# Last tokens of four batches multiplied as seven block products, and a new order of steps

## The chip, the core and the metric

The kernel runs on one core of a Trainium2 chip. The metric is device time of one execution in microseconds (us). A core has engines with queues of their own, each of which runs in the order written: TensorE (PE in the profile, with its weight loads as PEld), VectorE (DVE), ScalarE (ACT), GpSimd (POOL) and SyncE (SP), which only starts DMAs here. All arithmetic is in fp32.

## The reference

Eight batches of 576 tokens, 8 heads of 64 columns. Linear attention without a softmax, a normalisation of each head, then a gated unit with a causal convolution of 5 taps:

```
kv  = einsum('bhsd,bhse->bhde', k, v)
out = einsum('bhsd,bhde->bhse', q, kv)
x   = out / sqrt(mean(out*out, -1) + 1e-6) * g_norm      # heads joined: 576 x 512 per batch
gate = sigmoid(sum_k conv_w[k] * x[token - 4 + k])       # causal, per column
y   = (gate * (x @ w_val)) @ w_out                       # w_val, w_out: 512 x 512
```

## The kernel before

**Stages of one batch.** `kv_product` (PE) makes kv, `kv_copy` (ACT) takes it out of the PSUM bank. `load_q` and `turn_q` (SP, DVE) bring q turned over. `raw_pair` and `raw_tail` (PE, 64x64 tiles) multiply q by kv for chunks of 128 tokens, and for the last 64. `square` (ACT), `sums` (DVE) and `powers` (POOL) make the roots, `normalise` (ACT) scales the eight heads of a chunk. `turn_blocks` (DVE) turns the scaled chunk over in blocks and `move_blocks` carries four slices to x transposed (`xT`) by DMA, two from SP's queue and two from POOL's; the last 64 tokens go by `turn_x` (PE) and `keep_x` (ACT). `halo` (POOL) copies what the convolution needs from neighbours. `gate_start` (ACT), four `gate_tap` (DVE) and `gate_end` (ACT, sigmoid) make each of four column groups of the gate. `x_sums` (DVE), seven `val_fast` (PE) and `val_keep` (ACT and DVE) make x @ w_val from batch 2 on, as seven block products in place of eight. `gated` (DVE) multiplies by the gate; the product lies in `gv`.

**The output product.** Batches go in pairs i = 0 to 3. A batch's first 512 tokens are done in two groups of 256 tokens, so there are four groups p per pair. For each, a 2x2 block scheme takes seven products n = 0 to 6: `token_sums` (DVE) makes four sums of blocks of `gv` for both groups of a batch, `fast_product i p n` (PE) multiplies, `fast_keep` takes the results out of the banks: n = 0, 1, 2, 6 are ACT copies, n = 4 and 5 are DVE adds (n = 5 takes in product 3 as well). The last 64 tokens of both batches of a pair are multiplied plainly: `out_product i 8` (line 786) has 64 columns of weights on each half of the array, 512 columns wide, and `keep_out` copies the result. `store` sends each finished tile of 128 tokens with four DMAs. At the very end `store_part` and `store_last` split the last two tiles over SP's and ACT's queues.

**Order.** Nothing is scheduled automatically. `PLAN` is a list of some 1,250 steps, and each engine gets its instructions in the order of that list. `@ 1 4` behind a step names the buffers that it opens, out of rooms of fixed count (8 PSUM banks, 3 `w64` rooms for sums of tokens, 4 `ot` tiles for results, and so on). A wait arises where an engine reaches a step whose operands or buffer are not ready, and everything behind it on that engine waits too.

Of the kernel before, what the change touches and what calls it, by code (L numbers as in the profile page):

```python
# [43 lines left out]
narrow_weight wval 2 4; load_half k 2 1 @ 0; val_product 0 0 1 @ 2; keep_x 0 1; narrow_weight wout 1 5 @ 2;
keep_x 0 0; narrow_weight wval 2 7; narrow_weight wval 3 3; narrow_weight wout 1 0 @ 1;
narrow_weight wout 1 6 @ 0; gate_start 0 0 @ 0; kv_product 1 0; narrow_weight wval 3 4; gate_start 0 3 @ 1;
gate_tap 0 0 3; sort_q 1 2; turn_q_rows 1 4 @ 0; narrow_weight wval 3 7; val_product 0 0 0 @ 5; load_q 2 0;
gate_tap 0 0 2; keep_val 0 0 1; gate_tap 0 3 3; gate_start 0 1 @ 2; sort_q 1 4; val_sums 2;
val_product 0 3 0 @ 6; gate_tap 0 1 3; kv_copy 1 1; kv_copy 1 0; load_q 2 1; sort_q 1 0; gate_tap 0 0 1;
raw_tail 1 @ 0 2; gate_tap 0 3 2; raw_pair 1 3 @ 1 4; square 1 4 @ 2; narrow_weight wout 0 5 @ 3;  # L50
keep_val 0 0 0; gate_tap 0 0 0; val_product 0 2 1 @ 7; gate_start 0 2 @ 3; gate_tap 0 3 1; square 1 3 @ 0;
square 1 2 @ 1; sums 1 4 @ 1 1; gate_tap 0 2 3; narrow_weight wout 1 1; powers 1 4; load_half k 2 0 @ 0;
val_product 0 1 0 @ 5; sums 1 3; keep_val 0 1 1; stage_weight wout 3 @ 0; gate_end 0 0; gate_tap 0 1 2;
powers 1 3; narrow_weight wout 1 2; sums 1 2; narrow_weight wout 1 3; val_product 0 2 0 @ 3; gated 0 0;
keep_val 0 3 0; keep_val 0 2 1; gate_tap 0 2 2; normalise 1 4 @ 2; powers 1 2; narrow_weight wout 1 4;
normalise 1 3 @ 0; raw_pair 1 1 @ 7 6; turn_q 2 0 @ 0; stage_weight wout 2 @ 1; turn_q 2 2; turn_x 1 4 @ 0;
load_q 2 3; val_product 0 3 1 @ 2; gate_tap 0 3 0; keep_x 1 4; normalise 1 2 @ 1; gate_tap 0 2 1;
narrow_weight wout 0 6 @ 2; turn_x 1 3 @ 0; keep_val 0 3 1; gate_tap 0 1 1; load_q 3 1; turn_x 1 2 @ 1;
keep_val 0 1 0; square 1 1 @ 2; kv_product 2 0 @ 4 2; narrow_weight wout 0 0 @ 0; keep_x 1 3;
narrow_weight wout 1 7; keep_x 1 2; sums 1 1; kv_product 2 1; narrow_weight wout 0 1; gate_tap 0 1 0;  # L60
powers 1 1; square 1 0 @ 0; val_product 1 1 1 @ 5; narrow_weight wout 2 0 @ 1; load_half k 3 1 @ 0;
narrow_weight wout 0 2; narrow_weight wout 2 5 @ 1; load_half k 3 0 @ 0; narrow_weight wout 3 5 @ 3;
narrow_weight wout 0 3; sums 1 0; kv_copy 2 0; gate_tap 0 2 0; kv_copy 2 1; narrow_weight wout 2 1;
normalise 1 1 @ 2; powers 1 0; val_product 1 0 1 @ 0; narrow_weight wout 2 6 @ 0; narrow_weight wout 0 4;
turn_q 2 1; val_product 1 3 1 @ 1; halo 1; narrow_weight wout 2 2; narrow_weight wout 0 7; load_q 3 0;
keep_val 0 2 0; turn_q 2 3; keep_val 1 1 1; keep_val 1 0 1; weight_sums 0; normalise 1 0 @ 0; turn_x 1 1 @ 4;
load_q 3 2; narrow_weight wout 3 0 @ 0; raw_pair 2 3 @ 3 2; narrow_weight wout 3 6 @ 1; val_sums 0;
narrow_weight wout 2 3; raw_pair 2 1 @ 5 0; turn_q 3 1 @ 1; square 2 2 @ 1; turn_x 1 0 @ 6; square 2 3 @ 2;
narrow_weight wout 2 4; keep_x 1 1; val_product 1 2 1 @ 7; sums 2 2 @ 0 0; load_half v 3 0 @ 0; keep_x 1 0;
val_sums 1; gate_end 0 3; powers 2 2; load_half v 3 1 @ 0; sums 2 3; keep_val 1 3 1; gate_end 0 1; gated 0 3;  # L70
val_product 1 0 0 @ 4; gate_start 1 0 @ 0; narrow_weight wout 2 7; gate_end 0 2; powers 2 3; gated 0 1;
square 2 0 @ 0; gate_tap 1 0 3; val_product 1 1 0 @ 6; square 2 1 @ 1; turn_q 3 0; normalise 2 2 @ 1;
gated 0 2; load_q 3 3; val_product 1 2 0 @ 1; gate_tap 1 0 2; keep_val 1 2 1; keep_val 1 1 0; sums 2 1;
normalise 2 3 @ 2; load_q 4 0; turn_q 3 2; powers 2 1; val_product 1 3 0 @ 7; sums 2 0; narrow_weight wout 3 1;
token_sums 0 0 0 @ 2; keep_val 1 2 0; narrow_weight wout 3 2; turn_blocks 2 3; kv_product 3 0 @ 2 6;
powers 2 0; gate_tap 1 0 1; narrow_weight wout 3 3; token_sums 0 0 2 @ 1; keep_val 1 3 0;
fast_product 0 0 1 @ 3; normalise 2 1 @ 0; load_half k 4 0 @ 0; narrow_weight wout 3 4; token_sums 0 0 1;
fast_product 0 1 0 @ 1; turn_blocks 2 2; normalise 2 0 @ 2; fast_product 0 0 0 @ 7; turn_q 3 3; kv_product 3 1;
narrow_weight wout 3 7; load_q 4 2; fast_keep 0 0 1 @ 2; keep_val 1 0 0; token_sums 0 0 3; fast_keep 0 0 0 @ 3;
raw_tail 2 @ 0 5; gate_start 1 3 @ 1; turn_blocks 2 1; fast_product 0 0 3; square 2 4 @ 2; turn_blocks 2 0;  # L80
kv_copy 3 1; kv_copy 3 0; gate_start 1 1 @ 2; fast_product 0 1 1 @ 4; sums 2 4; move_blocks 2 0; weight_sums 1;
fast_keep 0 1 0 @ 0; raw_pair 3 1 @ 6 2; weight_sums 2; powers 2 4; gate_tap 1 1 3; move_blocks 2 2;
fast_product 0 0 2; gate_tap 1 0 0; move_blocks 2 1; fast_product 0 1 2; gate_tap 1 3 3; fast_keep 0 0 2;
fast_keep 0 1 1 @ 1; weight_sums 3; fast_product 0 0 5; move_blocks 2 3; fast_keep 0 1 2; gate_tap 1 1 2;
square 3 0 @ 1; fast_product 0 1 4; gate_end 1 0; sums 3 0 @ 1 1; load_q 4 1; square 3 1 @ 0;
fast_product 0 0 4; gate_tap 1 1 1; powers 3 0; gate_start 1 2 @ 3; fast_product 0 1 5; normalise 2 4 @ 1;
fast_keep 0 0 4; sums 3 1; fast_product 0 1 3; fast_keep 0 1 4; gate_tap 1 2 3; load_half v 4 1 @ 0;
powers 3 1; turn_x 2 4 @ 0; normalise 3 0 @ 0; fast_product 0 0 6; gate_tap 1 3 2; fast_product 0 1 6;
# [143 lines left out]
def kernel(  # L232
# [11 lines left out]
    nc = tc.nc  # L244
# [685 lines left out]
```

## Time and profile before

| | us |
|---|---|
| median of 3 runs (lowest, highest) | 295.53 (295.26, 296.04) |
| the profiled execution, its own time | 295.33 |
| its span in the trace | 293.5 |
| PE busy | 286.2 (98%) |
| DVE busy | 268.6 (91%) |
| ACT busy | 198.9 (68%) |
| POOL busy | 120.8 (41%) |

Busy time is a union over the engine's instructions. Mean durations are of single instructions, which overlap their neighbours a little, so a row of the chain (start, length, what) is the better price of a run of equal instructions. One matmul of the program is two matmul rows in the trace: a `fast_product` (two matmuls) is x4, an `out_product` (eight) is x16. L842 is `fast_product`, L748 `val_fast`, L786 `out_product`, L712 `gated`, L694 `gate_end`, L637 `normalise`, L755 `val_keep` on DVE, L618 `powers`, L817 `token_sums`, L853 `fast_keep` on DVE.

### The profile page before, as it was taken

To read this page: it belongs to the slowest core of one execution; us is meant where nothing else is said; L and a number is where in the kernel's file an instruction comes from. 1 tells how busy PE (TensorE), PEld (TensorE's weight loads), DVE (VectorE), ACT (ScalarE), POOL (GpSimd) and SP (SyncE) were. 2 spreads that over 40 slices of the span, in tenths; PEclk is the share of its full clock that TensorE was granted. 3 is DMA by queue.
4 is the path that set the end of the run, shared out by engine and by line. 5 is a ranking of instruction groups with operands and counts; after the bars stand their busy time and mean duration, and the time that the engine had idled before them with its cause. 6 is when DMAs were issued, how large, how long until landed. Compare 5 with 4: busy or idle time off the path is not lost.

```text
span 293.5 us, 8687 instructions
## 1 busy us (share of the span) xinstructions
PE 286.2 (98%) x3281; PEld 225.6 (77%) x3281; DVE 268.6 (91%) x484; ACT 198.9 (68%) x621; POOL 120.8 (41%) x131
## 2 busy tenths in 40 slices
PE   7999999999999999999999999999999999999994
PEld 3777778877887868878887767788887588888583
DVE  1699999999999999999999999999998999999812
ACT  2899999999786767776477576658588434723330
POOL 3067064754591478322981748031592072000020
PEclk9999999999999999999999999999999999999999
DMA  7999999878676856946699689624552170221344
GB/s 266 381 388 411 286 253 271 280 216 233 155 212 183 260 115 194 338 130 201 171 260 271 147 216 319 204 58 114 145 125 74 46 170 0 57 54 36 97 104 123
DMA packets 32201, 55.51 MB, mean 189 GB/s; under 512 B 6230, under 2 KB 14678, under 8 KB 32160
## 3 DMA queue, kind: packets, MB, share of 16 engines
q1 hardware_dynamic: 29424, 49.50, 57.5%
q0 software_dynamic: 1760, 3.43, 5.1%
q10 hardware_dynamic: 976, 2.03, 1.9%
q8 instruction: 26, 0.43, 0.6%
q14 instruction: 15, 0.12, 0.1%
HBM read 39.21 MB, written 9.44 MB: 166 GB/s over the span
## 4 chain that ended last, share of the span: by engine, by line
PE 77%; ACT 8%; DVE 7%; DMA 5%; issue 1%; DVEq 0%
PE bank L842 33%; PE bank L748 28%; PE bank L786 5%; PE bank L552 4%; PE bank L477 4%; ACT x L637 3%; DMA qs<-in_q_dram 3%; DVE gate L687 3%; DMA w<-in_moe_w_out_dram 2%; PE bank L564 2%; PE bank L516 1%; ACT gv L708 1%; DVE ss L608 1%; ACT sq L601 1%; DVE x L627 1%
## 5 line engine op out<-in xcount | busy, mean ns | idle before, releaser
L618 POOL TENSOR_TENSOR rt<-ss,mhalf 128x8 f32<-128x8 f32 (+3 forms) x38 | 73.1, 1937 | 81.1 <-DVE ss L608 81.0
L687 DVE SCALAR_TENSOR_TENSOR gate<-xT,cwT,gate 128x576 f32<-128x576 f32 x128 | 100.3, 806 | 0.2
L637 ACT ACTIVATE x<-bank,rt 128x64 f32<-128x64 f32 x252 | 56.0, 369 | 3.9 <-POOL rt L618 3.5
L842 PE MATMUL bank<-wsum,w 128*128 128x256 f32 x192 | 47.3, 381 | 0.0
L670 POOL DMA_DIRECT2D xT<-y x48 | 26.5, 557 | 41.4 <-DVE gv L755 13.5
L842 PEld LDWEIGHTS bank<-wsum,w 128*128 128x128 f32 x192 | 36.0, 190 | 6.1 <-issue 0.8
L748 PE MATMUL bank<-xs,vsum 128*128 128x288 f32 x144 | 37.1, 407 | 0.0
L748 PEld LDWEIGHTS bank<-xs,vsum 128*128 128x128 f32 x144 | 27.3, 190 | 7.3
L699 PE MATMUL bank<-xT,wval 128*128 128x288 f32 x128 | 32.5, 408 | 0.0
L842 PE MATMUL bank<-wout,gv 128*128 128x256 f32 x128 | 32.3, 382 | 0.0
L694 ACT ACTIVATE gate<-gate 128x576 f32<-128x576 f32 x32 | 23.0, 726 | 8.7 <-DVE gate L687 8.5
L699 PEld LDWEIGHTS bank<-xT,wval 128*128 128x128 f32 x128 | 23.7, 190 | 6.3 <-ACT xT L656 0.2
L842 PEld LDWEIGHTS bank<-wout,gv 128*128 128x128 f32 x128 | 24.0, 190 | 3.5
L681 ACT ACTIVATE gate<-xT,cwT 128x576 f32<-128x576 f32 x32 | 25.2, 805 | 1.0 <-DVE gv L712 1.0
L748 PE MATMUL bank<-xT,wval 128*128 128x288 f32 x96 | 25.7, 406 | 0.0
L601 ACT ACTIVATE sq<-bank 128x256 f32<-128x256 f32 (+1 forms) x70 | 21.7, 402 | 5.9 <-PE bank L552 5.7
L712 DVE TENSOR_TENSOR gv<-gv,gate 128x576 f32<-128x576 f32 x32 | 23.5, 745 | 2.0 <-ACT gate L694 1.5
L608 DVE TENSOR_REDUCE ss<-sq 128x8 f32<-128x520 f32 (+1 forms) x40 | 24.6, 621 | 0.3 <-ACT sq L601 0.3
L853 DVE TENSOR_TENSOR ot<-bank,ot 128x256 f32<-128x256 f32 (+1 forms) x33 | 17.3, 532 | 8.0 <-PE bank L842 4.0
L748 PEld LDWEIGHTS bank<-xT,wval 128*128 128x128 f32 x96 | 18.2, 190 | 4.5
L859 ACT COPY ot<-bank 128x256 f32<-128x256 f32 x16 | 6.1, 379 | 22.5 <-PE bank L842 22.5
L552 PEld LDWEIGHTS bank<-kv,qT 64*64 64x64 f32 x1008 | 16.3, 135 | 5.2 <-ACT x L637 2.8
(91 smaller groups left out, 468.1 us busy)
## 6 DMA issues: line engine op xcount, KB each, us to landing
qs<-in_q_dram SPq DMA_DIRECT2D x96, 140.0 KB, 4.0
out_dram<-ot SPq DMA_DIRECT2D x134, 64.0 KB, 1.7
k<-in_k_dram SPq DMA_DIRECT2D x14, 576.0 KB, 5.2
v<-in_v_dram SPq DMA_DIRECT2D x12, 576.0 KB, 5.3
xT<-y SPq DMA_DIRECT2D x48, 64.0 KB, 2.6
xT<-y POOLq DMA_DIRECT2D x48, 64.0 KB, 2.5
y<-in_moe_w_val_dram SPq DMA_DIRECT2D x4, 512.0 KB, 12.1
w<-in_moe_w_out_dram SPq DMA_DIRECT2D x4, 512.0 KB, 7.9
```

The lines of the kernel that those rows point to most:

```text
L552: nc.tensor.matmul(st["raw", b, c][r][cols, to * D:(to + 1) * D], st["qT", b][rows, hp, first:first + D], kvs[b % 2][rows, hp, :], start=T ...
L601: nc.scalar.activation(out=sq[:, r * n // 2:(r + 1) * n // 2, 0:D], in_=raw.rearrange("p (h e) -> p h e", e=D), func=AF.Square)
L608: nc.vector.reduce_sum(out=st["ss", b][:, FIRST[c]:FIRST[c] + n], in_=st["sq", b, c][:, 0:n], axis=AX.X)
L618: nc.gpsimd.tensor_tensor(out=st["rt", b][:, which], in0=st["ss", b][:, which], in1=mhalf[:, which], op=ALU.pow)
L637: nc.scalar.activation(out=x[:, to * D:(to + 1) * D], in_=raw[:, h * D:(h + 1) * D], func=AF.Copy, scale=root[:, to:to + 1])
L670: (nc.sync if i % 2 else nc.gpsimd).dma_start(out=xTs[b % 2][i * TB:(i + 1) * TB, :, first:first + P], in_=y[a * TB:(a + 1) * TB, i])
L681: nc.scalar.activation(out=gate[:], in_=xTs[b % 2][:, jt, HALO:SX], func=AF.Copy, scale=cwT[:, K - 1, jt:jt + 1])
L687: nc.vector.scalar_tensor_tensor(out=gate[:], in0=xTs[b % 2][:, jt, tap * TB:tap * TB + S], scalar=cwT[:, tap, jt:jt + 1], in1=gate[:], op ...
L699: nc.tensor.matmul(val[:], wval[:, kc, jt * P:(jt + 1) * P], xTs[b % 2][:, kc, HALO + n * SV:HALO + (n + 1) * SV], start=(kc == 0), stop=( ...
L712: nc.vector.tensor_tensor(out=both, in0=both, in1=st["gate", b, jt][:], op=ALU.mult)
L748: nc.tensor.matmul(st[bank, "val", b, mj][:], weights_[:, k], tokens()[:, k], start=(n in (0, 1, 3) and k == 0), stop=(k == NK // 2 - 1), ...
L842: nc.tensor.matmul(st[bank, i, p], tokens()[:, k], weights_[:, k], start=((n < 2 or n == 3 and ("bc", i, p) not in st) and k == 0), stop=( ...
```

## The change

The last tokens of pairs 2 and 3 (batches 4 to 7, 256 tokens together) are no longer multiplied by `out_product 2 8` and `out_product 3 8`. A new step `keep_tail b` (ACT) copies the 64 tokens of batch b out of `gv` into one of two new tiles, two batches to a tile of 128 tokens. The two tiles are the two token blocks of a fifth product, `fast_product 5 0 0` to `5 0 6`, with four `token_sums 5 0 n` of half the usual size. Its two result tiles are stored by `store_side`, that is, from POOL's queue. `move_blocks` becomes two steps, one for each queue, so that they can stand apart in the list. The first 211 steps are as before, and all steps behind them stand in another order, with other buffers. Pairs 0 and 1 keep their `out_product`.

```diff
-    def move_blocks(b, a):
+    def move_blocks(b, a, e):
...
-        for i in range(HB):
-            (nc.sync if i % 2 else nc.gpsimd).dma_start(
+        for i in range(1 - e, HB, 2):
+            (nc.gpsimd if e else nc.sync).dma_start(
...
+    def keep_tail(b):
+
+        i = b // 2
+        if ("tail", i) not in st:
+            st["tail", i] = new(("wexp", "wexp", "k0", "k1")[i], [P, NK, P], FP32, f"tail{i}")
+        first = b % GVS * S + SF
+        nc.scalar.copy(out=st["tail", i][:, :, b % 2 * T:(b % 2 + 1) * T], in_=gv[:, :, first:first + T])
...
-        block = lambda r, k: gv[:, k, begin:begin + SF].rearrange(
-            "p k (m r t) -> p k m r t", m=2, r=2)[:, :, :, r, :]
-        total = st["sums", i, h, n // 2][:, n % 2]
+        if i < B // 2:
+            block = lambda r, k: gv[:, k, begin:begin + SF].rearrange(
+                "p k (m r t) -> p k m r t", m=2, r=2)[:, :, :, r, :]
+            done = lambda m: st["sums", i, h, m // 2][:, m % 2]
+        else:
+            block = lambda r, k: st["tail", 2 * (i - B // 2) + r][:, k]
+            done = lambda m: st["sums", i, h, m // 2][:, m % 2, :, 0]
+        total = done(n)
...
-        chunk = lambda r, k: lambda: gv[:, k, begin + r * P:begin + (r + 1) * P]
+        chunk = lambda r, k: lambda: (
+            gv[:, k, begin + r * P:begin + (r + 1) * P] if i < B // 2 else st["tail", 2 * (i - B // 2) + r][:, k])
...
+            first = 2 * i
+            if i >= B // 2:
+                first, bb, n = 4 * (i - B // 2) + 2 * c, j // 2, NJ * HB + j % 2
+            queue.dma_start(out=rows_out[first + bb, n][:, cols], in_=ot[j * TB:(j + 1) * TB, cols])
```

The list's last stretch, from the last batch's last gates on. Before:

```
gated 7 0; fast_keep 3 0 1 @ 3; gate_end 7 1; fast_keep 3 0 4; fast_product 3 1 6; gate_tap 7 2 0; fast_product 3 0 6;
val_keep 7 1 3; fast_keep 3 1 6; gated 7 1; gate_end 7 3; fast_product 3 0 5; fast_keep 3 0 6; gated 7 3; gate_end 7 2;
store 3 1; fast_product 3 2 0 @ 2; val_keep 7 0 6; gated 7 2; fast_product 3 3 0 @ 4; fast_keep 3 1 5; store 3 3;
out_product 3 8 @ 5; fast_keep 3 0 5; token_sums 3 1 2 @ 0; token_sums 3 1 0 @ 1; store 3 2; fast_keep 3 2 0 @ 3; ...
```

After:

```
gated 7 0; gated 7 1; gate_end 7 3; gated 7 3; gated 7 2; fast_product 3 1 5; keep_tail 7; store 3 1;
token_sums 3 1 0 @ 1; fast_keep 3 0 5; token_sums 3 1 1; fast_product 3 2 0 @ 0; store 3 0; fast_product 3 3 0 @ 4;
fast_keep 3 1 5; store 3 2; token_sums 3 1 3 @ 2; fast_keep 3 2 0 @ 1; fast_product 3 2 1 @ 5; token_sums 5 0 0 @ 0;
... fast_keep 5 0 4; fast_keep 3 3 1 @ 0; fast_product 3 3 4; fast_product 5 0 6; fast_keep 3 3 4; store_part 3 7 1 0 0 2;
fast_keep 5 0 6; fast_product 3 3 6; fast_product 3 3 5; fast_keep 3 3 6; store_part 3 7 1 1 2 4;
store_part 3 7 0 0 0 2; fast_keep 3 3 5; store_side 5 1; store_part 3 7 0 1 2 4; fast_product 3 3 3 @ 2;
fast_keep 3 3 3; store_last 3 6 1; store_last 3 6 0
```

More of the change, by code (lines that the diff above doesn't have):

```diff
@@ L72 @@
[L72 to L76, printed above, removed]
@@ L117 @@
-val_fast 3 1 2; val_keep 3 1 3; gate_start 3 2 @ 2; turn_blocks 4 0; val_fast 3 1 1 @ 6; sums 4 2;
-gate_tap 2 1 1; powers 4 2; val_fast 3 0 4; val_keep 3 1 1; turn_blocks 4 3; val_keep 3 1 2; val_fast 3 1 5;
-gate_tap 2 1 0; gated 2 2; fast_product 0 2 5; gate_end 2 1; val_keep 3 1 5; fast_keep 0 3 6;
-normalise 4 2 @ 1; val_fast 3 1 4; gate_tap 2 3 0; store 0 7; fast_keep 0 2 5; val_fast 3 0 1 @ 6; turn_q 5 2;
-gate_end 2 3; kv_product 5 1 @ 0 5; x_sums 3 3 @ 3; gate_start 3 0 @ 1; gated 2 3; raw_tail 4 @ 7 2;
@@ L137 @@
-normalise 5 0 @ 1; sums 5 2; fast_product 1 0 5; gate_tap 3 0 1; val_fast 4 0 2; gate_tap 3 3 2;
-normalise 5 1 @ 2; val_fast 4 1 2; fast_keep 1 0 4; powers 5 2; gate_tap 3 3 1; load_half k 6 0 @ 0;
-fast_product 1 0 6; val_keep 4 0 2; x_sums 4 2 @ 1; val_keep 4 1 2; turn_blocks 5 1; val_fast 4 1 3 @ 2;
-fast_keep 1 0 6; load_half v 6 0 @ 0; fast_keep 1 0 5; val_fast 4 0 1 @ 5; gate_tap 3 1 0; gated 3 2;
-val_fast 4 0 4; val_keep 4 0 1; normalise 5 2 @ 0; gate_tap 3 3 0; val_fast 4 0 5; turn_q 6 0 @ 0;
@@ new lines @@
+gate_tap 1 3 3; square 3 3 @ 2; sums 3 3; square 3 2 @ 1; sums 3 2; turn_blocks 3 1; powers 3 3; store 0 2;
+gate_tap 1 2 2; fast_product 0 1 6; fast_keep 0 1 6; fast_product 0 0 6; x_sums 2 0 @ 0; gate_tap 1 2 1;
+gate_start 2 3 @ 0; fast_keep 0 0 6; normalise 3 0 @ 2; load_half k 4 0 @ 0; fast_product 0 0 3; halo 2;
+x_sums 2 1 @ 1; val_fast 2 1 0 @ 3; val_keep 2 1 0; kv_product 4 1 @ 5 0; kv_product 4 0; load_q 4 2;
+val_fast 2 0 0 @ 1; store 0 3; normalise 3 3 @ 1; gate_tap 1 2 0; powers 3 2; load_half v 5 1 @ 0; kv_copy 4 1;
@@ new lines @@
+raw_tail 4 @ 6 4; square 4 4 @ 1; kv_product 5 1 @ 2 7; kv_product 5 0; kv_copy 5 0; load_half v 6 1 @ 0;
+gate_tap 2 3 2; sums 4 4; powers 4 4; kv_copy 5 1; gate_tap 2 3 1; turn_blocks 4 0; gate_tap 2 3 0; normalise 4 4 @ 2;
+load_half k 6 1 @ 0; x_sums 3 1 @ 2; gate_end 2 3; val_fast 3 1 5; val_fast 3 0 5; move_blocks 4 3 0; turn_x 4 4 @ 2;
+gated 2 1; x_sums 3 2 @ 1; keep_x 4 4; val_fast 3 1 2; move_blocks 4 3 1; val_fast 3 0 2; load_half k 6 0 @ 0;
+turn_q 5 3; load_half v 6 0 @ 0; gate_start 3 0 @ 2; move_blocks 4 1 0; move_blocks 4 2 0; val_keep 3 1 2;
@@ new lines @@
+move_blocks 6 2 0; normalise 7 1 @ 0; normalise 7 3 @ 1; turn_blocks 7 2; fast_product 1 3 5; fast_keep 1 3 5;
+fast_product 1 2 6; fast_keep 1 2 6; x_sums 6 0 @ 2; fast_product 1 3 6; gate_start 6 3 @ 1; fast_keep 1 3 6;
+raw_tail 7 @ 6 0; square 7 4 @ 1; powers 7 0; gate_tap 5 1 0; turn_blocks 7 3; sums 7 4; x_sums 6 1 @ 0;
+val_fast 6 0 0 @ 5; gate_end 5 1; gated 5 1; fast_product 1 2 3; gate_tap 5 2 3; fast_product 1 2 5; powers 7 4;
+fast_keep 1 2 5; store 1 6; store 1 7; val_keep 6 0 0; normalise 7 0 @ 2; normalise 7 4 @ 1; gate_tap 5 2 2;
```

385 lines of the change are left out of this document (188 added, 197 removed).

## The prediction

> **What bounds the kernel now.** I read the page first, then the windows over stretches of my choice, then the chain. Columns of the windows: length, then busy time of PE, PEld, DVE, ACT and POOL with their instruction counts, clock, DMA share.
>
> ```profile
> span 293.5 us, 8687 instructions
> PE 286.2 (98%) x3281; PEld 225.6 (77%) x3281; DVE 268.6 (91%) x484; ACT 198.9 (68%) x621; POOL 120.8 (41%) x131
> 48.00:75.00 27.00, 26.72 (x509) 21.76 (x502) 27.00 (x51) 26.77 (x91) 14.17 (x10) 1.00 0.80 234
> 75.00:220.00 145.00, 145.00 (x1825) 117.07 (x1824) 144.08 (x248) 100.87 (x344) 76.75 (x81) 1.00 0.69 192
> 220.00:274.70 54.70, 54.70 (x256) 43.38 (x255) 52.22 (x85) 27.17 (x70) 9.45 (x18) 1.00 0.25 62
> 274.70:289.30 14.60, 14.60 (x67) 10.03 (x65) 6.17 (x11) 3.00 (x8) 2.05 (x4) 1.00 0.47 122
> 289.30:293.50 4.20, 0.00 (x1) 0.00 (x0) 0.42 (x1) 0.00 (x0) 0.00 (x0) 0.99 0.38 109
> ```
>
> The part whose order changes begins near 48 us. From there to 289.3 us PE lacks 0.28 us in all, so it sets the end. But DVE is almost as full: up to 274.7 us it is idle for 0.92 + 2.48 = 3.4 us out of 227. Only behind 274.7 us, when the last gates are done, has it room (8.4 us). ACT is full up to 75 us and free later. The clock is at 1.00, the DMA engines have room.
>
> The chain by time (start, length, what) prices PE's work.
>
> ```profile
> 120.78 0.86 PE bank L842 x4
> 205.41 12.28 PE bank L842 x56
> 227.39 3.58 PE bank L786 x16
> 231.38 2.14 PE bank L748 x8
> 268.90 1.94 PE bank L748 x8
> 275.16 3.58 PE bank L786 x16
> 278.74 10.57 PE bank L842 x48
> 289.31 0.02 issue
> 289.34 0.42 DVE ot L870
> ```
>
> A `fast_product` (x4) takes 0.86 us, an `out_product` 3.58 us. The last PE work ends at 289.31, and 4.2 us of copy, DMA and closing follow to 293.5.
>
> **The change, part by part.** *PE.* Two `out_product` go: 2 x 3.58 = 7.16 us. Seven `fast_product` come: 7 x 0.86 = 6.02. Net -1.14 us, all of it on the engine that sets the end. The two removed blocks also stand between work of other weight widths: L748 behind narrow-weight work took 2.14 us for x8, elsewhere 1.94, so one such border costs about 0.1 to 0.2 us; the last 12 products took 10.57 against 12 x 0.86 = 10.32. Each removed block had two borders, one of which may only move; I take -0.25 us, between 0 and -0.6. The Trainium skill ("TensorEngine Tiling (Array Packing)", Key Properties) says that a change of tiling mode drains the array; it names no price, and by it every border counts, which would be the -0.6 end.
>
> *DVE, ACT, queues.* Four half-size token sums and two result adds come to DVE, five copies net of two larger ones to ACT. The rows, by form (mean ns behind the busy time), and the DMA table:
>
> ```profile
> L853 DVE TENSOR_TENSOR ot<-bank,ot 128x256 f32<-128x256 f32 x18 | 7.4, 413 | 7.6 <-ACT ot L794 3.9 <-PE bank L842 3.6
> L853 DVE TENSOR_TENSOR ot<-bank,ot 128x512 f32<-128x512 f32 x15 | 10.1, 676 | 0.4 <-PE bank L842 0.4
> L859 ACT COPY ot<-bank 128x256 f32<-128x256 f32 x16 | 6.1, 379 | 22.5 <-PE bank L842 22.5
> L794 ACT COPY ot<-bank 128x512 f32<-128x512 f32 x4 | 2.4, 588 | 2.8 <-PE bank L786 2.8
> out_dram<-ot SPq DMA_DIRECT2D x134, 64.0 KB, 1.7
> out_dram<-ot SPq DMA_DIRECT2D x4, 32.0 KB, 1.7
> out_dram<-ot POOLq DMA_DIRECT2D x4, 64.0 KB, 1.9
> 282.72 2.05 POOL L882 DMA_DIRECT2D out_dram<-ot  x4 [36.83 <-ACT ot L855]
> ```
>
> The half-size sum isn't in the trace; its output is 256 elements like the first row, so between 0.41 us and the 0.68 of the full form, I take 0.41. DVE: 4 x 0.41 + 0.41 + 0.68 = 2.7 us, all behind the last gate in the new list, where DVE had 8.4 us free: cost nothing; without that cover 2.7 us. ACT: eight copies at 0.38 less two at 0.59 = 1.9 us, on an engine with 11.6 of its last 14.6 us free: nothing. The copies of batches 4 to 6 stand where ACT has half its time free. Stores: eight DMAs leave as before, now all eight from POOL. The last four wait for `fast_product 5 0 6`, behind which PE has three products (2.6 us). Copy 0.4, issue 2.05, landing 1.9 = 4.35: they land 1.8 us behind PE's end, inside the 4.2. The last DMAs behind PE's end are two on SP and two on ACT as before, of 64 KB in place of 32; both sizes show 1.7 us, so nothing, at most 0.1. `move_blocks` issues the same 96 DMAs; cut in two, SP's half no longer stands with POOL's, and neither waits for the other: nothing.
>
> *The new order.* It can't win PE more than the 0.28 us of idle time and a few borders, and it can lose any amount. What decides is DVE. I counted its steps: up to `gated 7 1` both lists give it the same 421 steps, so the same work. But behind the first two gates of batch 7, on which `fast_product 3 2 0` and all behind it hang, PE now has 14 + 6 = 20 products (17.2 us) to do; before it had 14 and one `out_product` (12.0 + 3.6 = 15.6, with borders 16.0 in the trace from 273.27 on).
>
> ```profile
> 220.21 0.74 DVE L733 TENSOR_TENSOR xs<-xT,xs 128x576 f32<-128x576 f32 x1
> 221.93 0.76 DVE L712 TENSOR_TENSOR gv<-gv,gate 128x576 f32<-128x576 f32 x1 [0.98 <-ACT gate L694]
> 250.00 0.76 DVE L712 TENSOR_TENSOR gv<-gv,gate 128x576 f32<-128x576 f32 x1 [0.49 <-ACT gate L694]
> 272.05 1.44 DVE L712 TENSOR_TENSOR gv<-gv,gate 128x576 f32<-128x576 f32 x2
> 273.27 1.89 PE L842 MATMUL bank<-wout,gv 128*128 128x256 f32 x8
> DVE gv L712 <- ACT gate L694: 1.5, 2, 1.0
> DVE gv L755 <- PE bank L748: 0.8, 3, 0.4
> ```
>
> Before, `gated 7 1` began at 272.05 and ended about 272.8. For PE to end at 289.31 - 1.39 = 287.9 these gates must be done by 287.9 - 17.2 = 270.7, which is 2.1 us earlier. DVE's idle time from 48 us up to there is 0.92 + 2.48 less the 0.45 behind it = 2.95 us, so two thirds must vanish. What speaks for it: 1.5 us of it is two waits of a `gated` for its sigmoid, and both have just one DVE step between last tap and gate (`x_sums 6 1`; `gated 6 2`). In the new list every gate has at least two steps between (least at `gated 6 0`: a `val_keep` and a `gated`, about 1.05 us, a distance that made no wait before). The 0.8 us of waits for `val_fast` can go as well, since the new list takes those results later. So 1.5 to 2.3 us go. Against that, the new list is tighter elsewhere (third rival). I take 1.6 us earlier: gates at 271.2, PE's end at 271.2 + 17.2 = 288.4.
>
> **The sum.** The profiled execution took 295.33 us: span 293.5 and 1.83 around it. PE's end moves from 289.31 to 288.4, which is -1.14 - 0.25 + 0.5 = -0.9, and 4.2 + 1.83 behind stay: 294.4 us. The profiled execution lies 0.2 below the median of 295.53; the three runs spread over 0.8, so I keep the sum as it is. About 0.3% (0.9 us) is what a measurement of this kernel can tell from no change.
>
> **Rivals.** *First: PE's saving is spent on the way.* DVE gets only as much idle time out as it puts in, the gates end near 272.3, and 272.3 + 17.2 + 4.2 + 1.83 = 295.5. From 271.5 to 272.9 this is within 0.3% (294.7 to 296.1). For it: DVE is idle for 0.92 us in the 145 us up to 220 and can't be had more closely; one new wait of 0.7 us decides.
>
> *Second: the full saving.* If DVE's waits go altogether, PE alone sets the end at 287.9, or 287.3 with all borders counted: 294.0 or 293.4.
>
> *Third, slower: DVE becomes the bound, by waiting in `turn_blocks`.* Between `sums` and `turn_blocks` of a chunk lie one `powers` and one `normalise`, while DVE does other steps.
>
> ```profile
> L618 POOL TENSOR_TENSOR rt<-ss,mhalf 128x8 f32<-128x8 f32 x29 | 58.0, 2013 | 54.1 <-DVE ss L608 54.0
> 64.42 1.64 ACT x L637 x8
> 70.87 3.31 ACT x L637 x16
> 76.06 0.42 DVE L608 TENSOR_REDUCE ss<-sq 128x4 f32<-128x260 f32 x1 [0.32 <-ACT sq L601]
> ```
>
> That path is 2.0 + 1.65 = 3.65 us when both queues are free, and a `powers` or `normalise` of another chunk ahead adds 2.0 or 1.65. The old list has 11 DVE steps or more in between (at some 0.63 us, 7 us), and DVE never waits there. The new one has 8 at chunks 5 2 and 4 2, 9 at 6 3, 10 at 6 2: 5 to 6.3 us. With one `powers` ahead (5.65) chunk 5 2 costs 0.6; with a `normalise` too (7.3) it costs 2.2, 4 2 about 1.8, 6 3 about 1.6. These waits all lie ahead of the gates. It decides from the point where gates end later than 272.05 (PE's old end less 17.2); two waits of 2 us against 1.8 us won put them at 273.1 to 275, which is 296.3 to 298. The stretch up to 75 us adds to it: ACT has 0.23 us free there, and the new list puts three steps more ahead of the last `normalise` of batch 2's full chunks (41 against 38, about 0.5 us). [...]
>
> That the seven products don't save at all is excluded by 3.58 against 0.86; only their place can spoil it.
>
> **Chances.** The forecast with the second rival, faster by over 0.3%: 0.43, of itself 293.3 to 294.6. The first, within 0.3%: 0.32. The third, slower by over 0.3%: 0.25, since both engines are full and every unforeseen wait of a whole new order goes to this side. The range takes in the first case and the second and the near part of the third: 293.3 to 296.7.
>
> **What would show it.** L786 x32 in place of x64, L842 x476 in place of x448 matmul rows; PE busy from 48 us on about 1.3 us less in sum with idle time still under 1 us; L712 waiting for L694 under 0.5 us; the first L842 behind the last gates starting near 271.3. Rival three would show as DVE idle ahead of L662, released by ACT L637, and PE waiting for L712 or L817. The forecast is wrong if DVE's idle time between 48 us and the last gates stays at 2.9 us or grows, or if the end behind the last product exceeds 4.4 us.

## The result, and the profile after

| | us |
|---|---|
| before, median (lowest to highest of 4 runs) | 295.39 (295.16 to 296.04) |
| after, median (lowest to highest of 4 runs) | 300.78 (297.48 to 302.06) |
| after over before, 95% interval | 1.0146 (1.0117 to 1.0175) |
| profiled execution of after, its span | 300.88, 299.1 |

The change makes the kernel slower, by 1.2 to 1.8%. (All ratios here leave out an execution that lies over 1.5% above the fastest of its kernel, as that of 302.06 does, while medians and ranges keep it; so the ratio is smaller than that of the medians.) The new kernel also scatters over more than 3 us, where the old one scatters under 1.

From the page of the changed kernel: the span, the busy shares, the chain's shares by engine and the gates on DVE. In the row of a group, the number behind the last bar is the engine's idle time ahead of it.

```profile
span 299.1 us, 8666 instructions
PE 286.8 (96%) x3277; PEld 228.3 (76%) x3277; DVE 271.1 (91%) x490; ACT 201.4 (67%) x627; POOL 118.4 (40%) x135
PE 58%; DMA 23%; SPq 6%; DVE 6%; ACT 2%; issue 1%; POOL 1%; ACTq 0%; DVEq 0%
L707 DVE TENSOR_TENSOR gv<-gv,gate 128x576 f32<-128x576 f32 x32 | 22.9, 741 | 0.0
```

The chain's shares before the change:

```profile
PE 77%; ACT 8%; DVE 7%; DMA 5%; issue 1%; DVEq 0%
```

DMA and SP's queue now hold 29% of the chain that ended last; before, it had 5% DMA. The gates (L707, before L712) wait for nothing any more: what the prediction watched went as it should. The time is lost elsewhere. The windows of the changed kernel, cut as before (length, then busy time of PE, PEld, DVE, ACT, POOL, clock, DMA share, GB/s):

```profile
48.00:75.00 27.00, 25.55 (x496) 20.41 (x491) 25.57 (x49) 26.20 (x91) 11.46 (x10) 1.00 0.93 262
75.00:220.00 145.00, 142.82 (x1824) 113.86 (x1824) 141.33 (x243) 100.81 (x346) 75.70 (x85) 1.00 0.69 186
220.00:274.70 54.70, 54.62 (x255) 44.98 (x254) 54.70 (x89) 29.11 (x73) 8.88 (x13) 1.00 0.27 68
274.70:293.40 18.70, 18.67 (x86) 15.79 (x84) 10.55 (x21) 4.35 (x13) 3.93 (x8) 1.00 0.34 87
293.40:299.10 5.70, 0.00 (x0) 0.00 (x0) 0.42 (x1) 0.00 (x0) 0.03 (x1) 0.82 0.31 86
```

PE, which was idle for 0.28 us between 48 us and its end, is now idle for 1.45 + 2.18 + 0.08 + 0.03 = 3.7 us. Idle time is not all of it: run 6 below, with nearly the same order and no late operands, has PE's end at 288.43 us, 4.95 us ahead of here, and only 3.6 us of that is idle time. The rest is work that takes longer behind a wait: in the chain of the changed kernel, four rows of L743 take 1.24 us at 120.64, directly behind a wait, and 0.97 us at 124.47. DVE's idle time up to 274.7 us went up, from 3.4 to 1.43 + 3.67 = 5.1 us, but it moved: none is left behind 220 us, all of it lies ahead. DMA is busier up to 75 us, 0.93 against 0.80. And behind PE's last work lie 5.7 us instead of 4.2. PE's end and what is behind it, out of the chain of the changed kernel:

```profile
54.86 11.15 DMA k<-in_k_dram
66.06 1.28 PE bank L472 x72
86.12 3.99 DMA k<-in_k_dram
90.25 1.28 PE bank L472 x72
173.69 5.33 DMA qs<-in_q_dram
272.47 20.91 PE bank L851 x96
293.40 0.42 DVE ot L862
```

The 24 last products run in one piece (20.91 us, 0.87 each) and end at 293.38, 4.07 us later than before. Twice in the early part a `kv_product` (L472) stands directly behind the landing of its own `k`. So of the 5.6 us that the span has grown, 4.1 lie ahead of PE's end and 1.5 behind it.

**The late operands.** Timeline rows of the changed kernel, PE and DVE; the bracket is the idle time ahead and what ended it:

```profile
50.02 0.43 DVE L413 TENSOR_SCALAR ot<-w 128x512 uint32<-128x512 uint32 x1 [1.24 <-DMA w<-in_moe_w_out_dram]
59.79 0.66 PE L644 MATMUL bank<-ident,x 128*128 128x128 f32 x4 [0.96 <-ACT x L632]
66.06 1.28 PE L472 MATMUL bank<-v,k 64*64 64x64 f32 x72 [0.49 <-DMA k<-in_k_dram]
179.04 0.76 DVE L728 TENSOR_TENSOR xs<-xT 128x576 f32<-128x576 f32 x1 [1.74 <-DMA qs<-in_q_dram]
```

The first row is `narrow_weight wout 2 5`: the new list puts it ahead of steps that it followed, its DMA lands at 49.9 us (49.7 before), DVE waits 1.24 us for it, and I read PE's wait 9 us later, for `normalise` in the second row, as the same delay handed on (run 6 tests that). The third is `kv_product 3 1`. In the list of before, the same step ran at 72.67 us, with both halves of `k` issued at 50.2. SP's queue, before and then after:

```profile
50.21 0.93 SPq L349 DMA_DIRECT2D k<-in_k_dram  x2
54.84 3.58 SPq L359 DMA_DIRECT2D qs<-in_q_dram  x8
...
72.67 1.28 PE L477 MATMUL bank<-v,k 64*64 64x64 f32 x72
```

```profile
50.98 1.26 SPq L344 DMA_DIRECT2D k<-in_k_dram  x1
52.34 0.41 SPq L344 DMA_DIRECT2D v<-in_v_dram  x1
52.85 1.97 SPq L354 DMA_DIRECT2D qs<-in_q_dram  x4
54.86 0.49 SPq L344 DMA_DIRECT2D k<-in_k_dram  x1
55.45 13.71 SPq L354 DMA_DIRECT2D qs<-in_q_dram  x12
```

Before, both halves of `k` stood ahead of q, the second 22 us ahead of its use; now it stands behind a v and four q issues, 11 us ahead, and with the engines fuller it took 11.15 us to land. The issues between 48 and 75 us with the median time to landing, before and after:

```profile
qs<-in_q_dram SPq DMA_DIRECT2D x23, 140.0 KB, 3.4
k<-in_k_dram SPq DMA_DIRECT2D x3, 576.0 KB, 4.7
v<-in_v_dram SPq DMA_DIRECT2D x2, 576.0 KB, 5.4
```

```profile
qs<-in_q_dram SPq DMA_DIRECT2D x24, 140.0 KB, 6.9
v<-in_v_dram SPq DMA_DIRECT2D x4, 576.0 KB, 7.1
k<-in_k_dram SPq DMA_DIRECT2D x3, 576.0 KB, 6.1
```

Seven loads of 576 KB stand there in place of five, and a q load takes twice as long. The Trainium skill ("DMA: Bandwidth & Descriptors", Issuing engines are not separate DMA queues) says that DMAs of all issuing engines share the same 16 DMA engines and interleave. The longer landing times here (q 6.9 us in place of 3.4) fit shared engines; as every load in these rows is SP's, they don't show the part about several issuing engines.

**The end.** POOL's stores in the changed kernel:

```profile
289.27 2.01 POOL L894 DMA_DIRECT2D out_dram<-ot  x4 [50.39 <-DVE ot L862]
291.47 1.96 POOL L894 DMA_DIRECT2D out_dram<-ot  x4 [0.20 <-issue]
```

Their last issue ends at 293.43. The raw trace has POOL's closing instruction (a DRAIN) end at 298.32, 4.9 us later, when SP's own closing waits had been through since 296.64. In the trace of before the last POOL issue ended at 284.77 and the closing at 289.33, 4.6 us later, hidden beside PE's last work.

My theory at this point had three parts: operands asked for earlier than their loads arrive, the weight copy among them; POOL's closing; and under both of them a new order that does save on PE. The rival was that the order itself is worse, that is, that any wait taken away comes back as another one on DVE or PE.

### The profile page after: what moved, and what is told of

It is laid out like the page before. It is cut to its first block, busy times and chain, and to the rows that moved or that the text cites. A ratio compares the mean times of both kernels' runs of the same rounds, so it can differ in the third digit from the quotient of the medians.

```text
span 299.1 us, 8666 instructions
## 1 busy us (share of the span) xinstructions
PE 286.8 (96%) x3277; PEld 228.3 (76%) x3277; DVE 271.1 (91%) x490; ACT 201.4 (67%) x627; POOL 118.4 (40%) x135
## 4 chain that ended last, share of the span: by engine, by line
PE 58%; DMA 23%; SPq 6%; DVE 6%; ACT 2%; issue 1%; POOL 1%; ACTq 0%; DVEq 0%
PE bank L851 26%; PE bank L743 23%; DMA qs<-in_q_dram 9%; DMA k<-in_k_dram 5%; DMA v<-in_v_dram 4%; DMA gv<-in_k_dram 4%; SPq L894 3%; PE bank L547 3%; PE bank L472 2%; DVE gate L682 2%; PE bank L694 2%; PE bank L781 1%; DMA out_dram<-ot 1%; SPq L378 1%; DVE xs L728 1%
## 5 line engine op out<-in xcount | busy, mean ns | idle before, releaser
L613 POOL TENSOR_TENSOR rt<-ss,mhalf 128x8 f32<-128x8 f32 (+3 forms) x38 | 69.5, 1844 | 68.6 <-DVE ss L603 67.3
L851 PE MATMUL bank<-wsum,w 128*128 128x256 f32 x204 | 49.4, 381 | 0.1
L851 PEld LDWEIGHTS bank<-wsum,w 128*128 128x128 f32 x204 | 38.2, 190 | 6.6 <-ACT ot L868 0.5
L743 PE MATMUL bank<-xs,vsum 128*128 128x288 f32 x144 | 38.5, 407 | 0.9 <-DVE xs L728 0.9
L689 ACT ACTIVATE gate<-gate 128x576 f32<-128x576 f32 x32 | 22.2, 693 | 17.5 <-DVE gate L682 17.1
L743 PEld LDWEIGHTS bank<-xs,vsum 128*128 128x128 f32 x144 | 27.0, 190 | 8.2 <-DVE xs L728 1.1
L694 PE MATMUL bank<-xT,wval 128*128 128x288 f32 x128 | 33.0, 410 | 0.0
L743 PE MATMUL bank<-xT,wval 128*128 128x288 f32 x96 | 27.1, 410 | 0.6 <-DVE ot L862 0.5
L596 ACT ACTIVATE sq<-bank 128x256 f32<-128x256 f32 (+1 forms) x70 | 21.1, 387 | 7.5 <-PE bank L547 7.0
L862 DVE TENSOR_TENSOR ot<-bank,ot 128x256 f32<-128x256 f32 (+1 forms) x35 | 18.5, 537 | 7.1 <-PE bank L851 6.4
L894 POOL DMA_DIRECT2D out_dram<-ot x8 | 4.0, 502 | 50.6 <-DVE ot L862 50.4
L707 DVE TENSOR_TENSOR gv<-gv,gate 128x576 f32<-128x576 f32 x32 | 22.9, 741 | 0.0
L743 PEld LDWEIGHTS bank<-xT,wval 128*128 128x128 f32 x96 | 17.9, 190 | 5.3 <-DVE ot L862 0.9
```

Source lines behind the costliest of these rows:

```text
L613: nc.gpsimd.tensor_tensor(out=st["rt", b][:, which], in0=st["ss", b][:, which], in1=mhalf[:, which], op=ALU.pow)
L689: nc.scalar.activation(out=gate[:], in_=gate[:], func=AF.Sigmoid)
L694: nc.tensor.matmul(val[:], wval[:, kc, jt * P:(jt + 1) * P], xTs[b % 2][:, kc, HALO + n * SV:HALO + (n + 1) * SV], start=(kc == 0), stop=( ...
L707: nc.vector.tensor_tensor(out=both, in0=both, in1=st["gate", b, jt][:], op=ALU.mult)
L743: nc.tensor.matmul(st[bank, "val", b, mj][:], weights_[:, k], tokens()[:, k], start=(n in (0, 1, 3) and k == 0), stop=(k == NK // 2 - 1), ...
L851: nc.tensor.matmul(st[bank, i, p], tokens()[:, k], weights_[:, k], start=((n < 2 or n == 3 and ("bc", i, p) not in st) and k == 0), stop=( ...
```

## The experiments

Runs of one group shared the runs of the kernel before, whose medians were 295.36 (runs 1 to 4), 295.37 (5 to 8), 295.21 (9 to 11) and 295.23 us (12); a comparison across groups carries that 0.16 us.

**1. The last tile from SP.**

```diff
-fast_keep 3 3 5; store_side 5 1; store_part 3 7 0 1 2 4;
+fast_keep 3 3 5; store 5 1; store_part 3 7 0 1 2 4;
```

> The changed kernel, with the last tile of the new product (store_side 5 1) sent from SP's queue, so that POOL's last DMA is that of tile 5 0. Theory (closing of POOL's queue): in the changed kernel POOL's closing drain ends 4.9 us behind its last DMA issue and holds the end of the program 1.7 us; here that issue is 2.2 us earlier, SP's last wait ends last again, and the time falls by 1.5 us (about 299.3 where the changed kernel has 300.8). Rival (the four late DMAs themselves make the end late, whichever queue sends them): no gain, or a loss of up to 1 us since SP gets four issues more just ahead of the last ones.

Measured: 298.76 us (297.17 to 302.96), ratio 1.0109 (1.0079 to 1.0139). In its profile PE ends at 292.3 and 4.9 us follow, against 5.7: the closing is worth 0.8 us here, and no more because four more stores now stand ahead of SP's last, which ends 2.4 us behind PE's end (before, 1.5). The rest of the difference lies in PE's earlier end, which scatters in this kernel.

**2 and 3. Both orders without the loads of q, k and v from batch 3 on** (the operands are left stale).

```diff
-        (nc.scalar if b == 0 and name == "v" else nc.sync).dma_start(out=t, in_=src)
+        if b < 3:
+            (nc.scalar if b == 0 and name == "v" else nc.sync).dma_start(out=t, in_=src)
...
-        for half in range(2):
+        for half in range(2) if b < 3 else ():
```

> The changed kernel, with the DMAs that load q, k and v left out from batch 3 on (those batches compute with what lies in the buffers). Theory (the new order asks for loads sooner than they arrive): PE's waits at 64, 88, 119 and 179 to 187 us vanish, 3 us or more in sum, of the 7.3 us that PE loses from 48 us on; about 297 to 297.5 us, with POOL's closing still there. Rival (the new order waits on ACT, POOL and DVE, whatever the loads do): within 1 us of the changed kernel, 300 to 301.

> The control: the kernel before, with the same loads left out from batch 3 on. Theory: its loads arrive in time, PE's sum sets the end, so it gains little: 294.5 to 295.4 us. Rival (loads cost every order alike, for instance through the traffic itself): it gains as much as the changed kernel does, 2 us or more.

Measured: the new order 297.56 us (297.23 to 298.07), the old one 295.20 (294.84 to 295.50; ratio 0.9995, 0.9986 to 1.0003). The loads cost the old order nothing and the new one about 3 us, and without them its scatter is gone too. What was left, 2.4 us, is for the next step.

**4. The old order with only the new tail.** `out_product 2 8` and `3 8` are taken out of the old list, and the seven products with their sums, copies and stores put in by hand, the last tile from SP.

```diff
-out_product 2 8; keep_out 2 8; store 2 8; ... out_product 3 8; keep_out 3 8; store_side 3 8
+keep_tail 4; keep_tail 5; keep_tail 6; ... keep_tail 7; fast_product 5 0 0; ... fast_product 5 0 6; store 5 1
```

> The old order, with the seven products of the last tokens of batches 4 to 7 in place of the two plain ones: only the tail's steps and the stretch behind the last gates are written anew; the last tile goes from SP's queue. If PE's sum alone decides: 1.1 to 1.4 us less than before, about 294.1. If the last gates decide (they end at 272.8 us and 20 products of 0.86 us follow): PE ends at 290.1, about 296.2 us, 0.8 more than before.

Measured: 304.50 us (304.14 to 305.01), ratio 1.0312 (1.0299 to 1.0325), which neither side expected. Most of it is my own tail: ACT stood 5.3 us for a result tile whose earlier contents were the last of four tiles in SP's queue (`store` 3 1, 3 3, 3 2, 3 0), and PE behind it 4.8 us. Behind that wait the granted clock was 0.50 from 282 to 286 us, and two products took 3.6 us in place of 1.7. So this run doesn't settle whether the new tail alone would pay in the old order. But one row of it tells something else. PE at the place where `out_product 2 8` stood, before and in this kernel:

```profile
227.32 3.65 PE L786 MATMUL bank<-wout,gv 128*64 128x512 f32 x16
231.31 1.24 PE L748 MATMUL bank<-xs,wval 128*128 128x288 f32 x4
```

```profile
227.50 0.48 PE L549 MATMUL bank<-kv,qT 64*64 64x64 f32 x16
229.30 1.24 PE L745 MATMUL bank<-xs,wval 128*128 128x288 f32 x4 [1.32 <-DVE xs L730]
```

With the 3.65 us gone, PE reaches the next product only 2.0 us earlier, since DVE's `x_sums` isn't done: in the old order the removed block was cover for DVE. That part of a new order is needed.

**5. The price of POOL's closing by itself**: the kernel before, with its last two issues from POOL.

```diff
-        store(i, c, nc.scalar if n else nc.sync, range(begin, end), HIGH if half else LOW)
+        store(i, c, nc.scalar if n else nc.gpsimd if not half else nc.sync, range(begin, end), HIGH if half else LOW)
```

> The kernel before, unchanged but for its very last two issues (lower half of the last tile), which go from POOL instead of SP. PE's end should stay at 289.3 us. Theory of the closing drain: in the profile of the changed kernel POOL's closing ended 4.9 us behind its last issue, in that of before 4.6 us, where an SP issue needs about 1.8 us to land. POOL's last issue would end near 291 us here, so the closing would end near 295.7 and the span near 296.5 instead of 293.5: about 298.3 us, +3.0. Rival (only the landing of the store counts, which is 1.9 us from POOL against 1.7 from SP): +0.2 us, 295.6.

Measured: 298.34 us (297.96 to 298.52), ratio 1.0101 (1.0088 to 1.0114). That is the +3.0 of the theory. POOL's last row and the windows behind PE's end:

```profile
289.66 0.98 POOL L882 DMA_DIRECT2D out_dram<-ot  x2 [5.28 <-DVE ot L870]
289.30:291.50 2.20, 0.00 (x0) 0.00 (x0) 0.07 (x1) 0.00 (x0) 0.98 (x2) 1.00 0.65 181
291.50:296.20 4.70, 0.00 (x0) 0.00 (x0) 0.00 (x0) 0.00 (x0) 0.00 (x0) 0.69 0.00 0
```

In the last 4.7 us nothing computes and no byte moves: the data has landed, and the program waits for POOL to close (its closing instruction ends at 295.37, 4.7 us behind its last issue).

**6. The new order without loads, with the other two parts mended.** The weight copy stands four instructions of DVE later, and the last tile goes out half from SP and half from ACT.

```diff
-square 1 0 @ 0; narrow_weight wout 2 5 @ 3; narrow_weight wout 0 0 @ 0; ... turn_q 2 1;
+square 1 0 @ 0; narrow_weight wout 0 0 @ 0; ... turn_q 2 1; narrow_weight wout 2 5 @ 3;
...
-        store(i, c, nc.gpsimd)
+        if c == 0:
+            store(i, c, nc.gpsimd)
+        else:
+            store(i, c, nc.scalar, range(2, 4))
+            store(i, c, nc.sync, range(0, 2))
```

> The changed kernel without the loads of q, k and v from batch 3 on (those operands are left stale), with two more edits: the narrowing copy of the weight block wout 2 5, which waited 1.9 us for its DMA on DVE, stands behind turn_q 2 1; and the last tile of last tokens goes out two blocks from SP and two from ACT instead of four from POOL. The same kernel without these two edits took 297.56 us. Theory (everything that was lost is loads asked for early, the weight copy asked for early, and the closing of POOL): 297.56 - 1.5 to 1.7 (PE's wait at 59 us) - 1.6 to 1.9 (closing) = 294.0 to 294.5, below the 295.2 of the old order without loads. Rival (the new order itself is worse on DVE, the wait only moves on): 296 or more.

Measured: 294.33 us (294.23 to 294.72), ratio to the kernel before 0.9969 (0.9957 to 0.9981), as the theory expected. The spans and the last PE piece of the three kernels without loads: new order, new order mended, old order; for the first two also the window up to 75 us.

```profile
span 295.7 us, 8513 instructions
48.00:75.00 27.00, 25.44 (x507) 20.45 (x500) 25.14 (x49) 25.60 (x90) 11.46 (x10) 1.00 0.04 11
269.07 20.91 PE bank L852 x96
```

```profile
span 292.5 us, 8514 instructions
48.00:75.00 27.00, 27.00 (x573) 21.87 (x564) 26.64 (x51) 27.00 (x95) 11.44 (x10) 1.00 0.04 12
267.52 20.91 PE bank L854 x96
```

```profile
span 293.7 us, 8533 instructions
279.06 10.57 PE bank L843 x48
```

PE ends at 289.98, 288.43 and 289.63; behind it lie 5.7, 4.1 and 4.1 us. So the weight copy cost 1.55 us at PE's end, as much as PE's idle time up to 75 us (1.56, now nothing); the closing cost 1.65; and with both mended the new order is 0.9 us faster than the old one in the same condition (294.33 against 295.20).

**7. The same two edits with all loads.**

> The changed kernel with the two edits alone (weight copy wout 2 5 behind turn_q 2 1; last tile from SP and ACT). Theory: 298.76 (last tile from SP) - 1.0 (issues shared out) - 1.1 (weight copy) = 296.7. Rival (the loads take back what the weight copy gives, since kv_product 3 only comes to wait longer for its k): 297.7.

Measured: 298.05 us, twelve runs from 295.37 to 301.62, ratio 1.0078 (1.0051 to 1.0104). The rival was nearer: of the 2.1 us that the theory expected from the two edits, 0.7 came. PE at `kv_product 4 0` in its profile:

```profile
90.44 1.28 PE L474 MATMUL bank<-v,k 64*64 64x64 f32 x72 [1.22 <-DMA k<-in_k_dram]
```

With the run before, the loads' price in the new order is 298.05 - 294.33 = 3.7 us, and with them comes the scatter: 6.2 us against 0.5.

**8. Four steps that meet a late load, moved later.**

```diff
-kv_product 3 0 @ 6 0; kv_product 3 1; ... kv_copy 3 0; ... kv_copy 3 1; ... fast_product 0 1 1 @ 7;
+kv_product 3 0 @ 6 0; ... kv_copy 3 0; ... fast_product 0 1 1 @ 7; kv_product 3 1; kv_copy 3 1;
-kv_product 4 0; load_q 4 2; val_fast 2 0 0 @ 1;    turn_q 5 2 @ 1; ... gate_tap 2 0 0;    x_sums 5 0 @ 2; gate_tap 4 3 3;
+load_q 4 2; val_fast 2 0 0 @ 1; kv_product 4 0;    ... gate_tap 2 0 0; turn_q 5 2 @ 1;    gate_tap 4 3 3; x_sums 5 0 @ 2;
```

> The changed kernel with all loads, the two edits (weight copy later, last tile from SP and ACT), and four steps of the order moved by one or two places, so that they ask for their operand about 0.9 us later: kv_product 3 1 behind fast_product 0 1 1, kv_product 4 0 behind val_fast 2 0 0, turn_q 5 2 behind gate_tap 2 0 0, x_sums 5 0 behind gate_tap 4 3 3. Theory (each wait is a local appointment with a late load, and 0.4 to 1.0 us of lateness goes with it): 300.8 or, with the last tile from SP, 298.8; less 1.1 (weight copy), 1.0 (closing, SP's issues shared out), 0.6 + 0.5 + 0.7 + 0.5 (the four appointments): 294.4 to 296. Rival (the DMA engines are the bound in 48 to 75 us, busy 0.93 of it, and what one wait gives back the next takes): as the run with the two edits alone, within 0.5 us.

Measured: 297.35 us (296.37 to 299.46), ratio 1.0077 (1.0050 to 1.0103). In this order `kv_copy 3 0` reads its bank before the second half is added, and `kv_product 3 1` then waits 0.45 us for that copy instead of for its `k`, so the run is no clean test of this one step. Against run 7 it is 0.7 us lower in the median, no difference in the ratio: nearer to the rival.

**9. Two loads earlier in SP's queue**, with `turn_q 5 2` and `x_sums 5 0` moved as in 8.

```diff
-load_half k 3 0; turn_q 3 1; ... load_half v 3 1; load_q 3 0; ... load_half k 3 1;
+load_half k 3 0; load_half k 3 1; turn_q 3 1; ... load_half v 3 1; load_q 3 0;
-move_blocks 2 0 0; ... store 0 2; ... load_half k 4 0;
+move_blocks 2 0 0; load_half k 4 0; ... store 0 2;
```

> The changed kernel with the two edits (weight copy later, last tile from SP and ACT: 298.05 us, twelve runs from 295.4 to 301.6), and with two loads issued earlier in SP's queue (k 3 1 directly behind k 3 0, ahead of v 3 1 and q 3 0; k 4 0 behind the block moves of batch 2, ahead of a store that waits for DVE), and turn_q 5 2 and x_sums 5 0 one step later. Theory (the waits come from when a load gets onto the queue and from what shares the engines with it): kv_product 3 1 loses 0.3 instead of 1.0 us, kv_product 4 0 nothing instead of 1.4, x_sums 5 0 nothing instead of 0.5: 295.3 to 296.0, the spread within 2 us. Rival (the DMA engines are full in 48 to 75 us, any order of the same loads loses as much there): 297.5 or more, with the wait only at another load.

Measured: 297.43 us (296.15 to 298.60), ratio 1.0075 (1.0052 to 1.0098). The windows and one row of PE:

```profile
48.00:75.00 27.00, 27.00 (x569) 21.89 (x561) 26.64 (x51) 27.00 (x95) 11.44 (x10) 1.00 0.96 291
75.00:220.00 145.00, 142.46 (x1764) 113.28 (x1763) 141.57 (x244) 100.62 (x347) 74.48 (x85) 1.00 0.66 181
87.73 0.48 PE L744 MATMUL bank<-xT,wval 128*128 128x288 f32 x1 [1.45 <-DMA qs<-in_q_dram]
```

Up to 75 us PE now loses nothing, with the DMA engines at 0.96, as full as in run 7, where PE is idle for 0.9 us in this stretch. So full engines alone aren't the price; it matters which transfer is late. But behind 75 us PE is idle for 2.5 us: the early load of `k 4 0` lies beside the block moves of batch 2, and `val_fast 2 1 0` waits instead. (The row names a q load as what ended the wait, but this product reads no q. Of the block moves that it reads, the last two were issued at 82.1 and 82.7 us and took 4.8 us to land, where the median is 2.4. That the load of `k` made them late is my reading.) The total is the rival's.

**10. `kv_product 3`, both halves and copies, behind `fast_product 0 1 1`**, on top of the edit of 9.

> As the run above, with both halves of kv_product 3 and their copies one step later, behind fast_product 0 1 1 (about 0.9 us). Theory: what is left of the wait for k 3 goes, less what fast_product 0 1 1 then waits for its own operand: 0.3 us under the run above, 295.0 to 295.7. Rival: fast_product 0 1 1 waits as long as kv_product 3 did: the same as the run above.

Measured: 298.81 us (298.45 to 303.15), ratio 1.0117 (1.0103 to 1.0132): worse than 9, which neither side expected. Its one profile is of the execution of 303.15 us, 4 us above the next, so I don't read a cause from it.

**11. The two edits of 6, without the q loads only** (from batch 3 on q is left stale).

> The changed kernel with the two edits, without the loads of q from batch 3 on (q is left stale; k and v are loaded): of the 576 and 560 KB transfers a third falls away, and k and v keep their place in the order. With all loads it took 298.05, with none 294.33. Theory (k and v come late because the engines are full and the q loads ahead of them hold SP's queue): most of the 3.7 us goes, 294.5 to 295.5, and the runs agree within 1 us. Rival (k and v are late by their own place in the order, 576 KB each behind the rooms that kv_product 2 frees): 297 or more, with the waits at kv_product 3 1 and 4 0 as they were.

Measured: 295.63 us (294.19 to 297.98), ratio 1.0020 (1.0000 to 1.0039). Of the 3.7 us, 2.4 go with the q loads, although no load of k or v was moved. The median is 0.1 above what the theory allowed, and the runs still scatter over 3.8 us where it expected 1. The window up to 75 us:

```profile
48.00:75.00 27.00, 27.00 (x569) 21.89 (x561) 26.65 (x51) 27.00 (x95) 11.45 (x10) 1.00 0.49 166
```

**12. Block moves ahead of loads that can wait**, on top of 9.

```diff
-load_half v 4 1; ... move_blocks 2 0 0; load_half k 4 0;      load_half k 5 0; ... load_half v 5 0; ... move_blocks 3 0 0;
+load_half v 4 1; load_half k 4 0; ... move_blocks 2 0 0;      ... move_blocks 3 0 0; load_half k 5 0; load_half v 5 0;
-load_half k 6 0; ... load_half v 6 0; ... move_blocks 4 0 0;  load_half v 7 0; ... move_blocks 5 3 0;
+... move_blocks 4 0 0; load_half k 6 0; load_half v 6 0;      ... move_blocks 5 3 0; load_half v 7 0;
```

> As the run with two loads moved (297.43 us; in its profile val_fast 2 1 0 lost 1.6 us to block moves of batch 2 that landed late beside the load of k 4 0, and val_fast 4 0 0 and the product behind it 1.2 us to those of batch 4), with k 4 0 ahead of batch 2's block moves (behind v 4 1) and with the loads that nobody needs for 20 us or more behind the block moves of their time: k 5 0 and v 5 0 behind those of batch 3, k 6 0 and v 6 0 behind those of batch 4, v 7 0 behind those of batch 5. Theory (the loss is the order in which loads and block moves share SP's queue and the engines): both waits fall to 0.5 us or less, 297.43 - 2.3 = 295.1, between 294.6 and 295.6, the runs within 1.5 us: level with the kernel before, and 0.8 above the same order without loads. Rival (the same bytes have to go in the same time, so another transfer is late): 297 or more.

Measured: 298.97 us (297.58 to 299.49), ratio 1.0113 (1.0094 to 1.0132). The rival holds. Both waits of run 9 are gone, and DVE waits for q instead:

```profile
116.70 0.71 DVE L497 STREAM_TRANSPOSE qT<-qs 128x512 f32<-128x512 f32 x1 [2.13 <-DMA qs<-in_q_dram]
```

No version with all loads beat the kernel before.

## Why the prediction was wrong, point by point

**PE's own work: right in kind, somewhat too large.** Forecast were -1.14 and -0.25 for borders, in sum -1.4. With the loads gone and the two other parts mended, PE ends at 288.43 against 289.63 in the old order: -1.2. But the profiled execution of the old order was the slowest of its ten (295.50); by the medians the gain is 0.9 us (295.20 to 294.33, with 4.1 us behind PE's end in both). So no run here shows the 0.25 for borders. In the changed kernel itself PE's busy time from 48 us on rose, from 241.0 to 241.7 us, where 1.3 us less was forecast; its waits hide the saving. That PE's end agrees with the forecast's 288.4 is luck: the forecast had 0.5 us for late gates, and there they cost nothing (the four last gates run from 269.02 to 271.77 us, so the first two end near 270.4 where 271.2 was forecast, and the last products run unbroken); this made up for a saving that was taken too large.

**DVE's gates: right about their waits, and not what decided.** L712's 2.0 us of waits became 0.0 at L707. Rival three's place was wrong: `turn_blocks` (L657) has 0.0 us of idle time ahead of it. Its sign was right, its mechanism did not happen; nor did the first rival's, since PE's last 24 products ran unbroken. Two slips in the working changed nothing: the second rival's 287.3 counts the borders twice (289.31 - 1.14 - 0.6 is 287.6, hence 293.6 us), and the copies that ACT gained are six net, not five (627 instructions against 621).

**"The DMA engines have room": this is the step that failed first.** It was read from shares of 0.80 and 0.69 and then dropped. The sum moved the work of PE, DVE, ACT and POOL, and gave SP's loads no term at all, though the new list moved nearly all of them behind its 211th step, and the steps that consume them. What a row of before would have told is the distance: `k` for batch 3 issued at 50.2 us and used at 68.7 and 72.7, and the list of after has `kv_product 3 1` 30 steps sooner and the load of its `k` 52 steps later, behind four issues of q. The missing term measured 3.7 us (298.05 against 294.33).

**The same step on a small scale: `narrow_weight wout 2 5`.** I compared DVE's steps up to `gated 7 1` by count (421 in both) and concluded "the same work". A count says nothing of when operands land. The term measured 1.55 us at PE's end without the other loads; with them much of it goes to the next late load (run 7 against run 1: 0.7 us for both edits, less than the scatter).

**The stores from POOL, "inside the 4.2 ... nothing": wrong by 1.5 us.** I took the landing of a POOL store (1.9 us) as its end. The queue's closing is what counts, 4.9 us behind the last issue. Shown by run 5 (+3.0 us for two issues moved to POOL in the old kernel) and by run 6 (4.1 us behind PE's end in place of 5.7).

**The sum of the parts.** From run 6: 294.33 + 3.7 (loads) + 1.55 (weight copy) + 1.65 (closing) = 301.2, against 300.78 measured. This tests the last two terms only, as the 3.7 is itself run 7 less run 6, and with a kernel that scatters by 3 us it is a weak test. The condition that I wrote for the forecast to be wrong (DVE's idle time at 2.9 us or more, more than 4.4 us behind the last product) came true on both counts: 5.1 and 5.7. The chance of 0.25 for slower was too small for a list in which nearly every load had moved.

**What stays open.** Whether some order of the loads would keep the 0.9 us with all bytes moving. Runs 9 and 12 removed the waits that they aimed at and had others in their place; 8 and 10 aimed at waits too, and all four ended between 297.3 and 299.0. Run 9 against run 11 shows that neither the engines' share nor one particular load is the cause by itself; that the new list leaves too little time between load and use in many places fits all the runs, but I only argued it and didn't try an order with that time restored throughout. Nor did I find why run 10 was slower than run 9.

## What to carry to other kernels

When a list of steps is reordered, price the loads as well as the engines: for each one, when it gets onto its queue, when it is used, and how long its landing takes in that stretch when one or two more transfers share it. A transfer share of 0.8 was not room here once the new order left a load 11 us between issue and use in place of 22. And a store from POOL at the end of this program cost its queue's closing, not its landing: let POOL's last issue be well ahead of the last compute (4.5 us ahead cost nothing in the kernel before, and 2.1 us ahead nothing in runs 1 and 6).

## What the hardware showed that I had not expected

In every trace of this case POOL's closing ends 4.6 to 4.9 us behind its last DMA issue, and 4.7 us of a span can pass with no byte moving and no engine busy (run 5). The program whose transfers land just in time scattered by 6 us (run 7, 295.4 to 301.6), and the same program without those transfers by 0.5 (run 6): here scatter went with waits for DMA. Within one execution of the changed kernel one 576 KB load took 3.99 us to land and another 11.15.
